# The sign of a double joined to its exponent: an integer and / or on VectorE in place of ScalarE's sign and a bf16 product

## The chip, the cores and the metric

The kernel runs on one core of a Trainium2 chip. The core has five engines that run side by side: TensorE (PE, matmuls, with its weight loads shown as PEld), VectorE (DVE), ScalarE (ACT), GpSimd (POOL) and SyncE (SP, which here issues the DMA transfers). The metric is device time in microseconds (us) of one launch, as the median of several runs. The profile of one further launch shows where that time goes.

## The reference

A recurrent attention over 768 steps feeds a gated feed-forward network. The matrices of the network are drawn as float64, so each of their numbers reaches the chip as 8 bytes.

```python
for t in range(S):                                   # B, H, S, D = 4, 8, 768, 40
    y[:, :, t] = np.einsum('bhd,bhde->bhe', rt, state)
    Sa = np.einsum('bhde,bhe->bhd', state, at)
    state_decay = state * wt[:, :, None, :] - np.einsum('bhd,bhe->bhde', Sa, bt)
    state = state_decay + np.einsum('bhd,bhe->bhde', vt, kt)
...
a = x @ w1                                           # x: 3072 x 320, w1, w2: 320 x 1024
b = x @ w2
h = a * b @ w3                                       # w3: 1024 x 1024
return (h @ w_out).astype(np.float32)                # w_out: 1024 x 320
```

## The kernel before

**Stages.** The sequence is cut into 12 chunks of 64 steps. Of each chunk the kernel makes: scaled inputs (`scale`: L438, L443, L459, L463, L467, L455), the products among its steps (`causal`: L492 on PE, `JP` and `lh` copies on ACT), the inverse of a triangular matrix on VectorE (`solve`: it begins with the transpose L524 and goes through some 50 products and sums, L550 and L554, to the transposes L599 and L602), the join of its halves (`join`: L625 and L632 on PE), then for four groups the recurrence itself (`rec`: L719, L726, L735, L748 on PE, L740, L772, L792 on VectorE), and at the end the network on the chunk's 256 tokens (`mlp`: `xs` is split into two parts by L827 and L830, L844 is x times w1 and w2, L858 the product of the two, L861 and L205 its two parts `gl` and `gh`, L870 the product with the last matrix).

**The weights' conversion.** Before the first `mlp` can start, the float64 weights have to become float32 on the chip. `convert` does this for a piece of 128 x 512 numbers; there are 31 pieces. A piece is loaded as 64-bit integers into `raw` (L317). L320 shifts the sign and exponent's 16 bits right by 4 and keeps 11 of them in `e`; L324 on ACT turns these into the bits of a bf16 power of two, still in `e`; L327 on ACT takes the sign of the 16-bit integer into `sg` (bf16); L330 and L334 on VectorE build the mantissa in `mf` (float32) from the two 32-bit halves; L338 multiplies sign and power (both bf16) into `sg`; L341 multiplies `mf` by it. What comes out is copied (`split`: ACT L205 and VectorE L383, L395 make the two parts of w1 and w2 in `W`), or feeds `product`, which multiplies w3 and w_out on PE once (L405, eight times 8 products) and splits the result into `W3h` and `W3l` (L205 and L410). The last pieces of `W` release the marker `W12`, which the first `xs` and L844 wait for.

**What sets the order.** Every engine works off one fixed list. `Order.place` makes these lists before the launch: it goes through all operations with a cost and a due time each, gives each to its engine at the earliest free time, picks by due time among those that can start, and gives out buffers (`SLOTS`) in the same pass. Operations with `two=True` are kept from running on VectorE and POOL at the same time in that plan. Strings in `ON` say for each piece whether L338 (`cb`, 26 d and 5 p) and L341 (`cv`, 9 d and 22 p) go to VectorE (d) or POOL (p). A changed cost or dependency in `convert` therefore changes the order of everything near it.

Of the kernel before, what the change touches and what calls it, by code (L numbers as in the profile page):

```python
# [8 lines left out]
F32 = mybir.dt.float32  # L9
F32R = mybir.dt.float32r  # L10
BF16 = mybir.dt.bfloat16
U16, I16 = mybir.dt.uint16, mybir.dt.int16
I32, U32, I64 = mybir.dt.int32, mybir.dt.uint32, mybir.dt.int64
AF = mybir.ActivationFunctionType
ALU = mybir.AluOpType
# [14 lines left out]
CW = 512  # L30
LAT = dict(pe=0.33, act=0.09, dve=0.09, pool=0.1, sp=2.4, nil=0.0)
SLOTS = dict(rc=2, fm=8, al=4, lh=6, gi=2, gt=1, ab=1, TDX=1, rv=3, xu=3, bk=3, hs=2, st=2, y=1, xr=1, JP=2, TT=2, bank=6,
             raw=4, e=3, sg=3, mf=4, w3f=3, xs=1, gh=1, gl=1, ga=2, o=2)


ENGINES = tuple(getattr(mybir.EngineType, n) for n in ("PE", "Activation", "DVE", "Pool", "SP"))
# [2 lines left out]
         ga=6.52, ml=90.63, kp=1.61, mt=25.46, mg=10.0)  # L39

ON = dict(cv="ppdpppdppppdddppppdpppppdddpppp", ws="d", lh="pppppppppppp", xs="dppppppppppp", gl="ppppppppppdd",
          cb="dddddddddddddddddddpdpddddddppp")
# [15 lines left out]
class Order:  # L58
# [11 lines left out]
    def slot(self, pool):  # L70
        return Slot(self, pool)

    def op(self, eng, cost, due, fn, r=(), w=(), two=False, kind=None, hold=(), dma=0.0):
        if self.direct:
            fn()
            return
        n, deps = len(self.ops), set()
        for k in r:
            deps.add(self.written.get(k))
            self.read.setdefault(k, []).append(n)  # L80
        for k in w:
# [112 lines left out]
def attention_moe(ctx: ExitStack, tc: tile.TileContext, fmx, fma, rv, vt, sq, svr, w12, w12c, w3t, wo, out):  # L194
    nc = tc.nc
    pe, act, dve, pool = nc.tensor, nc.scalar, nc.vector, nc.gpsimd
# [15 lines left out]
    for q in range(2):  # L212
        r = slice(64 * q, 64 * q + 64)
# [55 lines left out]

    cv, pp = ExitStack(), ExitStack()  # L270
    cvp = cv.enter_context(tc.tile_pool(name="cv", bufs=1, side="right"))
    for name, n, dt in (("raw", CW, I64), ("e", CW, U16), ("sg", CW, BF16), ("mf", CW, F32)):
        tiles[name] = [cvp.tile([128, n], dt, name=f"{name}{i}") for i in range(SLOTS[name])]
    ppp = pp.enter_context(tc.tile_pool(name="pp", bufs=1))
    wof = ppp.tile([128, NJ, DM], F32, name="wof")
# [16 lines left out]
    op, slot = order.op, order.slot  # L292
# [16 lines left out]
    def convert(src, dst, due, w=()):  # L309

        n = src.shape[1]
        raw, e, sg, mf = slot("raw"), slot("e"), slot("sg"), slot("mf")
        k = count[0]
        count[0] += 1

        def f1():
            sp.dma_start(out=raw.t[:, 0:n], in_=src)  # L317

        def f2():
            dve.tensor_scalar(out=e.t[:, 0:n], in0=raw.t.bitcast(U16)[:, 3:4 * n:4], scalar1=4, scalar2=0x7FF,  # L320
                              op0=ALU.logical_shift_right, op1=ALU.bitwise_and)

        def f3():
            act.activation(e.t[:, 0:n], e.t[:, 0:n], AF.Relu, scale=128.0, bias=ebias)  # L324

        def f4():
            act.activation(sg.t[:, 0:n], raw.t.bitcast(I16)[:, 3:4 * n:4], AF.Sign)  # L327

        def f5():
            dve.tensor_scalar(out=mf.t.bitcast(I32)[:, 0:n], in0=raw.t.bitcast(I32)[:, 1:2 * n:2], scalar1=0xFFFFF,  # L330
                              scalar2=0x100000, op0=ALU.bitwise_and, op1=ALU.bitwise_or)

        def f6():
            dve.scalar_tensor_tensor(out=mf.t[:, 0:n], in0=raw.t.bitcast(U32)[:, 0:2 * n:2], scalar=2.0 ** -32,  # L334
                                     in1=mf.t.bitcast(I32)[:, 0:n], op0=ALU.mult, op1=ALU.add)

        def f7(x):
            x.tensor_tensor(out=sg.t[:, 0:n], in0=sg.t[:, 0:n], in1=e.t[:, 0:n].bitcast(BF16), op=ALU.mult)  # L338

        def f8(e):  # L340
            e.tensor_tensor(out=mf.t[:, 0:n] if dst is None else dst(), in0=mf.t[:, 0:n], in1=sg.t[:, 0:n], op=ALU.mult)  # L341

        op("sp", 0.4, due - 8, f1, w=[raw], dma=2.0)
        op("dve", 0.42, due, f2, r=[raw], w=[e], two=True)
        op("act", 0.73, due, f3, w=[e])
        op("act", 0.67, due, f4, r=[raw], w=[sg])
        op("dve", 0.38, due, f5, r=[raw], w=[mf], two=True)
        op("dve", 0.62, due, f6, r=[raw], w=[mf], two=True)
        both(ON["cb"][k], 1.2, 0.38, due, f7, r=[e], w=[sg])
        both(ON["cv"][k], 1.25, 0.62, due, f8, r=[sg, "conv"], w=[mf] if dst is None else [mf, *w])  # L350
        return mf

    def weights():

        due, step = P["w0"], P["ws"]
        for k in range(3):
            if k == 1:
                for f in range(NJ * DM // CW):
                    cs = slice(CW * f, CW * f + CW)
                    convert(wo[:, cs], lambda cs=cs: wof.rearrange("p j n -> p (j n)")[:, cs], due, w=["wof"])  # L360
                    due += step
                for ib in range(NJ):
                    w3f = slot("w3f")
                    for f in range(1024 // CW):
                        cs = slice(CW * f, CW * f + CW)
                        convert(w3t[ib, :, cs], lambda w3f=w3f, cs=cs: w3f.t[:, cs], due, w=[(w3f, f)])
                        due += step
                    product(ib, w3f, due)
                op("nil", 0.0, due, second, w=["reg2"])
            for f in range(2048 // CW if k < 2 else DFF // CW):  # L370
                cs = slice(CW * f, CW * f + CW)
                due = split(k, f, cs, due)
                due += step
        op("nil", 0.0, due, third, r=[("W", k, f) for k in range(3) for f in range(4)], w=["W12", "conv"])

    def split(k, f, cs, due):

        over = ["conv"] if k == 0 else ["conv", "reg2"]
        if k < 2:
            mf = convert(w12[k * 128:k * 128 + 128, cs], None, due)  # L380

            def f2(e):
                e.tensor_tensor(out=WT[2 + k][:, cs], in0=mf.t, in1=WT[k][:, cs], op=ALU.subtract)  # L383

            op("act", 0.65, due, lambda: copy(WT[k][:, cs], mf.t), r=[mf, *over], w=[("W", k, f)])
            both(ON["ws"], 1.35, 0.62, due, f2, r=[mf, *over], w=[("W", k, f)])
            return due
        mf = convert(w12c[:, cs], None, due)
        for h in range(2):
            q, dst = slice(64 * h, 64 * h + 64), slice(DFF * h + CW * f, DFF * h + CW * f + CW)  # L390
            key = ("W", 2, 2 * h + f)
            for o in range(h + 1):
                op("act", 0.65, due, lambda q=q, dst=dst, o=o: copy(WT[4][64 * o:64 * o + 64, dst], mf.t[q]),
                   r=[mf, *over], w=[key])
            both(ON["ws"], 1.35, 0.62, due, lambda e, q=q, dst=dst: e.tensor_tensor(  # L395
                out=WT[4][64:128, dst], in0=mf.t[q], in1=WT[4][q, dst], op=ALU.subtract), r=[mf, *over], w=[key])
        return due
# [557 lines left out]
    for i in list(nc.cur_bb.bb.instructions)[begun:]:  # L955
        if i.engine in ENGINES:
            if i.engine in behind:
# [10 lines left out]
                      op1=ALU.is_equal)  # L968
# [78 lines left out]
```

## Time and profile before

| | |
|---|---|
| median of 3 runs | 756.51 us (756.47 to 760.34) |
| the profiled execution | 756.74 us, of which the span from first to last instruction 755.0 us |
| PE busy | 608.8 us (81%) |
| VectorE busy | 579.6 us (77%) |
| ACT busy | 480.3 us (64%) |
| POOL busy | 290.7 us (39%) |

The span is what the engines' rows cover; the 1.7 us beyond it lie around it. In the prediction's rows, a group of instructions reads: line, engine, operation, names written and read, shapes, how many, then busy time in us, the mean duration of one in ns, and the idle time before them with what ended it. A row of the timeline begins with its start in us and its duration in us; an instruction's successor on the same engine can start before that duration is over, so the step from start to start is what a row costs its engine.

### The profile page before, as it was taken

What the parts mean: (1) busy time and instruction counts of PE and PEld (TensorE: products, weight loads), DVE (VectorE), ACT (ScalarE), POOL (GpSimd) and SP (SyncE); (2) the same over time, 40 slices, a digit from 0 to 9 for tenths busy, and PEclk for the clock granted to TensorE, in tenths of its full rate; (3) what the DMA queues carried; (4) which work ended last, traced back from release to release, by engine and by line L of the source; (5) the groups of instructions that cost most, each with busy time, mean ns of one, the idle gap of its engine ahead of it and who ended that gap; (6) DMA issues with size and microseconds to landing.
All of it is one profiled execution on the core that took longest, in us unless ns stands there. A gap on an engine that the chain in (4) does not pass through costs nothing.

```text
span 755.0 us, 23802 instructions
## 1 busy us (share of the span) xinstructions
PE 608.8 (81%) x9458; PEld 525.1 (70%) x9458; DVE 579.6 (77%) x1317; ACT 480.3 (64%) x1309; POOL 290.7 (39%) x374
## 2 busy tenths in 40 slices
PE   1312199658689899898898998998989989999996
PEld 1211176336579788797787887977878779788996
DVE  6969999899885895985968959859589498693421
ACT  3744466458857668768676687686767776836431
POOL 3155414534443363443533634435426244321000
PEclk9999999877779999999999999999999999999999
DMA  7833264134220312313113233142232231211010
GB/s 181 223 90 96 81 184 143 44 123 135 62 51 15 97 51 70 88 44 98 50 51 96 50 74 83 46 97 53 54 89 57 63 80 46 55 28 44 8 35 20
DMA packets 67554, 57.63 MB, mean 76 GB/s; under 512 B 31600, under 2 KB 58480, under 8 KB 67440
## 3 DMA queue, kind: packets, MB, share of 16 engines
q1 hardware_dynamic: 67440, 56.08, 27.9%
q8 instruction: 76, 1.25, 0.7%
q14 instruction: 38, 0.31, 0.1%
HBM read 47.40 MB, written 3.93 MB: 68 GB/s over the span
## 4 chain that ended last, share of the span: by engine, by line
DVE 31%; PE 21%; ACT 18%; issue 6%; SPq 3%; DMA 1%; POOL 0%; DVEq 0%; ACTq 0%; POOLq 0%
PE bank L844 8%; DVE tmp L550 6%; ACT JP L205 5%; ACT TT L205 4%; DVE xu L740 3%; PE bank L870 3%; PE bank L748 3%; SPq L802 3%; PE bank L492 2%; DVE ab L524 2%; DVE DG L554 2%; ACT xu L205 2%; DVE fm L443 2%; DVE ga L858 2%; DVE Tp L554 2%
## 5 line engine op out<-in xcount | busy, mean ns | idle before, releaser
L844 PE MATMUL bank<-xs,W 128*128 128x256 f32 x1536 | 205.5, 288 | 2.3 <-issue 1.7
L844 PEld LDWEIGHTS bank<-xs,W 128*128 128x128 f32 x1536 | 188.4, 190 | 10.3 <-issue 3.7
L740 DVE TENSOR_TENSOR xu<-bank,mask_h 64x208 f32<-64x208 f32 x192 | 71.2, 371 | 57.7 <-PE bank L735 54.5
L467 POOL TENSOR_TENSOR fm<-fm,gi 104x512 f32<-104x512 f32 x44 | 62.7, 1425 | 117.0 <-DVE gi L463 91.2
L205 ACT ACTIVATE xu<-bank 64x128 f32<-64x128 f32 (+2 forms) x368 | 90.7, 297 | 19.0 <-PE bank L669 9.2
L205 ACT ACTIVATE JP<-bank 32x256 f32<-32x256 f32 (+1 forms) x216 | 75.7, 350 | 38.2 <-PE bank L492 34.8
L510 POOL TENSOR_SCALAR_AFFINE_SELECT lh<-lh 64x256 f32<-64x256 f32 x96 | 39.9, 415 | 129.6 <-ACT lh L205 125.8
L455 POOL TENSOR_TENSOR lh<-al,fm 104x512 f32<-104x512 f32 x48 | 59.5, 1245 | 43.5 <-PE bank L726 32.5
L748 PE MATMUL bank<-xu,bk 128*40 128x104 f32 (+1 forms) x768 | 49.6, 262 | 24.2 <-DVE xu L740 24.2
L726 PE MATMUL bank<-xu,lh 104*64 104x104 f32 (+2 forms) x768 | 53.2, 272 | 17.4 <-ACT xu L205 9.1
L861 POOL TENSOR_TENSOR gl<-ga,gh 128x512 fp32r<-128x512 f32 x40 | 51.5, 1286 | 32.8 <-ACT gh L205 32.8
L679 POOL TENSOR_SCALAR_AFFINE_SELECT xu<-xu 64x256 f32<-64x256 f32 x96 | 41.2, 429 | 57.7 <-ACT xu L205 49.6
L870 PE MATMUL bank<-W3h,gh 128*128 128x320 f32 x192 | 63.2, 329 | 0.0
L748 PEld LDWEIGHTS bank<-xu,bk 128*40 128x40 f32 (+1 forms) x768 | 37.4, 118 | 34.0 <-DVE xu L740 29.0
L726 PEld LDWEIGHTS bank<-xu,lh 128*64 128x64 f32 (+2 forms) x768 | 41.4, 145 | 27.9 <-ACT xu L205 16.5
L870 PE MATMUL bank<-W3l,gh 128*128 128x320 f32 x192 | 59.3, 309 | 0.0
L870 PE MATMUL bank<-W3h,gl 128*128 128x320 f32 x192 | 59.1, 308 | 0.0
L205 ACT ACTIVATE gh<-ga 128x512 fp32r<-128x512 f32 x48 | 30.1, 628 | 38.1 <-DVE ga L858 37.8
L447 ACT ACTIVATE gi<-fm 104x256 f32<-104x256 f32 x48 | 20.0, 416 | 53.7 <-DVE fm L443 51.2
L694 PE MATMUL bank<-ident,fm 104*128 104x104 f32 x192 | 28.8, 277 | 29.9 <-DMA al<-in_fma_dram 11.6
L405 PE MATMUL bank<-wof,w3f 128*128 128x320 f32 x128 | 44.2, 497 | 6.4 <-POOL w3f L341 6.2
L492 PE MATMUL bank<-lh,fm 40*64 40x64 f32 x1536 | 38.8, 238 | 12.8 <-POOL fm L467 8.3
(102 smaller groups left out, 1297.5 us busy)
## 6 DMA issues: line engine op xcount, KB each, us to landing
fm<-in_fmx_dram SPq DMA_DIRECT2D x48, 313.6 KB
raw<-in_w3t_dram SPq DMA_DIRECT2D x16, 512.0 KB
rv<-in_rv_dram SPq DMA_DIRECT2D x96, 80.0 KB
raw<-in_w_dram SPq DMA_DIRECT2D x8, 512.0 KB
al<-in_fma_dram SPq DMA_DIRECT2D x96, 40.0 KB
xu<-in_vt_dram SPq DMA_DIRECT2D x96, 40.0 KB
out_dram<-o SPq DMA_DIRECT2D x48, 80.0 KB
xr<-y SPq DMA_DIRECT2D x72, 40.0 KB
```

The lines of the kernel that those rows point to most:

```text
L205: act.activation(out_, in_, AF.Copy, scale=scale)
L405: pe.matmul(out=pt.t[:, 0:DM], lhsT=w[:, j], rhs=wof[:, j], start=(j == 0), stop=(j == NJ - 1))
L455: e.tensor_tensor(out=lh.t[0:104], in0=al.t.unsqueeze(1).to_broadcast(full), in1=gam(c, g)[:, :, 0:C].unsqueeze(1).to_broadcast(full), op= ...
L467: e.tensor_tensor(out=X, in0=X, in1=gi.t.unsqueeze(2).to_broadcast([104, NP, 2, C]), op=ALU.mult)
L492: pe.matmul(out=bank(ab)[64 * x:64 * x + 64, p], lhsT=X[r, p, x], rhs=lh.t[r, ab, p], start=True, stop=True)
L550: dve.tensor_tensor(out=scratch(*shape), in0=x().to_broadcast([128, *shape]), in1=y().to_broadcast([128, *shape]), op=ALU.mult)
L726: pe.matmul(out=view(hp)[64 * ab:64 * ab + 64, p], lhsT=lh.t[k, ab, p], rhs=xu.t[k, ab, p], start=True, stop=True)
L740: dve.tensor_tensor(out=xu.t[64 * ab:64 * ab + 64, ab, k:NP:2], in0=qs[ab].t[r, 256:256 + 2 * N].rearrange("p (n t) -> p n t", n=2), in1=m ...
L748: pe.matmul(out=q(r, p), lhsT=bk.t[:, p, r], rhs=xu.t[:, ab, p], start=(c == 0), stop=True, skip_group_check=True)
L844: pe.matmul(out=pt.t[:, TOK * x:TOK * x + TOK], lhsT=WT[k][:, cs], rhs=xs.t[:, z], start=(n == 0), stop=(n == 7))
L861: both(ON["gl"][c % NCH], 1.35, 0.62, t + 1, lambda e, a=a, j=j: e.tensor_tensor(out=gl.t[:, j:j + 2], in0=a.t, in1=gh.t[:, j:j + 2], op=A ...
L870: pe.matmul(out=pt.t[:, 0:DM], lhsT=l.t[:, j, ts], rhs=W3[r][:, j], start=(j == 0 and n == 0), stop=(j == NJ - 1 and n == 2))
```

## The change

`convert` keeps L320 (shift and mask) and L324 (the bf16 power of two). ACT's L327 and the tile `sg` go. In place of L338 there is one `scalar_tensor_tensor` on VectorE (L336 of the changed kernel) that takes the top 16 bits of each number from `raw`, ands them with 0x8000 and ors them into `e`. The final product (L340 of the changed kernel) reads `e` as bf16 instead of `sg`. All 31 of the new instructions are on VectorE; `cb` is no longer read. `e` has four buffers in place of three, and each is held until the final product. Line numbers of the changed kernel are smaller from here on: L330 has become L327, L334 L331, L341 L340, and after `convert` each is smaller by 1.

```diff
-             raw=4, e=3, sg=3, mf=4, w3f=3, xs=1, gh=1, gl=1, ga=2, o=2)
+             raw=4, e=4, mf=4, w3f=3, xs=1, gh=1, gl=1, ga=2, o=2)
...
-        def f4():
-            act.activation(sg.t[:, 0:n], raw.t.bitcast(I16)[:, 3:4 * n:4], AF.Sign)
...
-        def f7(x):
-            x.tensor_tensor(out=sg.t[:, 0:n], in0=sg.t[:, 0:n], in1=e.t[:, 0:n].bitcast(BF16), op=ALU.mult)
-
-        def f8(e):
-            e.tensor_tensor(out=mf.t[:, 0:n] if dst is None else dst(), in0=mf.t[:, 0:n], in1=sg.t[:, 0:n], op=ALU.mult)
+        def f7():
+
+            dve.scalar_tensor_tensor(out=e.t[:, 0:n], in0=raw.t.bitcast(U16)[:, 3:4 * n:4], scalar=0x8000,
+                                     in1=e.t[:, 0:n], op0=ALU.bitwise_and, op1=ALU.bitwise_or)
+
+        def f8(x):
+            x.tensor_tensor(out=mf.t[:, 0:n] if dst is None else dst(), in0=mf.t[:, 0:n],
+                            in1=e.t[:, 0:n].bitcast(BF16), op=ALU.mult)
...
-        op("act", 0.67, due, f4, r=[raw], w=[sg])
...
-        both(ON["cb"][k], 1.2, 0.38, due, f7, r=[e], w=[sg])
-        both(ON["cv"][k], 1.25, 0.62, due, f8, r=[sg, "conv"], w=[mf] if dst is None else [mf, *w])
+        op("dve", 0.62, due, f7, r=[raw], w=[e], two=True)
+        both(ON["cv"][k], 1.25, 0.62, due, f8, r=[e, "conv"], w=[mf] if dst is None else [mf, *w])
```

The lists of all engines change up to the third chunk's network. Three places show how.

VectorE's list early in the conversion (names are tiles with buffer numbers), before:

```order
L467 TENSOR_TENSOR fm_99<-fm_99,gi_115 104x512
L338 TENSOR_TENSOR sg_168<-sg_168,e_165 128x512
L320 TENSOR_SCALAR e_166<-raw_162 128x512
L330 TENSOR_SCALAR mf_172<-raw_162 128x512
L334 SCALAR_TENSOR_TENSOR mf_172<-raw_162,mf_172 128x512
L338 TENSOR_TENSOR sg_169<-sg_169,e_166 128x512
```

and the same place now:

```order
L466 TENSOR_TENSOR fm_99<-fm_99,gi_115 104x512
L336 SCALAR_TENSOR_TENSOR e_165<-raw_161,e_165 128x512
L320 TENSOR_SCALAR e_166<-raw_162 128x512
L327 TENSOR_SCALAR mf_170<-raw_162 128x512
L331 SCALAR_TENSOR_TENSOR mf_170<-raw_162,mf_170 128x512
L442 SCALAR_TENSOR_TENSOR fm_100<-fm_100,first 104x260
L336 SCALAR_TENSOR_TENSOR e_166<-raw_162,e_166 128x512
```

L336 stands where L338 stood, with `raw` as an input more, and a scan of the next group (L442) has moved between the two.

VectorE's list where the weights are done and the first `xs` is made (row 376 of it before), before:

```order
L772 TENSOR_TENSOR st_130<-bank_154,fm_103 104x80
L395 TENSOR_TENSOR W_4_1599<-mf_173,W_4_1599 64x512 x2
L459 TENSOR_TENSOR gt_116<-fm_100,gi_114 104x256
L463 SCALAR_TENSOR_TENSOR gi_114<-gt_116,gi_114 104x256
L443 SCALAR_TENSOR_TENSOR fm_101<-fm_101,first 104x260
L830 TENSOR_TENSOR xs_1852<-xr_132,xs_1852 128x768
L792 TENSOR_TENSOR y_131<-bank_156,fm_103 104x2x64
L792 TENSOR_TENSOR y_131<-bank_154,fm_103 104x2x64
```

and now (row 388):

```order
L771 TENSOR_TENSOR st_130<-bank_157,fm_103 104x80
L791 TENSOR_TENSOR y_131<-bank_156,fm_103 104x2x64
L791 TENSOR_TENSOR y_131<-bank_157,fm_103 104x2x64
L549 TENSOR_TENSOR tmp<-ab,DG 128x256
L394 TENSOR_TENSOR W_4_1512<-mf_171,W_4_1512 64x512 x2
L458 TENSOR_TENSOR gt_116<-fm_101,gi_115 104x256
L462 SCALAR_TENSOR_TENSOR gi_115<-gt_116,gi_115 104x256
L442 SCALAR_TENSOR_TENSOR fm_102<-fm_102,first 104x260
L829 TENSOR_TENSOR xs_1852<-xr_132,xs_1852 128x768
```

Counted over the whole list ahead of the first `xs`, seven instructions that stood behind it stand ahead of it now: one each of L443, L459, L463, L550 and L554 (256 elements) and two L792; all else is the same but for `convert`'s own. On PE, sixteen L492 rows have moved ahead of the first L844 in the same way.

PE's list at the join of the chunk whose recurrence follows the second `mlp`, before:

```order
L870 MATMUL bank_156<-W3h,gl_1851 128x320
L632 MATMUL bank_155<-TDX_117,JP_134 32x32 x32
L870 MATMUL bank_156<-W3h,gh_1850 128x320
L870 MATMUL bank_156<-W3l,gh_1850 128x320
L870 MATMUL bank_156<-W3h,gl_1851 128x320
L870 MATMUL bank_156<-W3h,gh_1850 128x320
L870 MATMUL bank_156<-W3l,gh_1850 128x320
L870 MATMUL bank_156<-W3h,gl_1851 128x320
L719 MATMUL bank_153<-rv_118,SB 64x104
```

and now:

```order
L869 MATMUL bank_156<-W3h,gh_1850 128x320
L869 MATMUL bank_156<-W3l,gh_1850 128x320
L869 MATMUL bank_156<-W3h,gl_1851 128x320
L631 MATMUL bank_155<-TDX_117,JP_134 32x32 x32
L718 MATMUL bank_152<-rv_118,SB 64x104
```

The six products between the join's second half and the recurrence's first step have moved ahead. From that L719 on, the kinds and sizes of instructions on PE stand in the same order in both kernels to the end (4623 matmuls of 6164); so they do on VectorE (807 of 1309), ACT and POOL from near the same point, and every list has the same instructions ahead of it but for `convert`'s.

More of the change, by code (lines that the diff above doesn't have):

```diff
@@ L271, in attention_moe @@
     cvp = cv.enter_context(tc.tile_pool(name="cv", bufs=1, side="right"))
-    for name, n, dt in (("raw", CW, I64), ("e", CW, U16), ("sg", CW, BF16), ("mf", CW, F32)):
+    for name, n, dt in (("raw", CW, I64), ("e", CW, U16), ("mf", CW, F32)):
         tiles[name] = [cvp.tile([128, n], dt, name=f"{name}{i}") for i in range(SLOTS[name])]
@@ L311, in convert @@
         n = src.shape[1]
-        raw, e, sg, mf = slot("raw"), slot("e"), slot("sg"), slot("mf")
+        raw, e, mf = slot("raw"), slot("e"), slot("mf")
         k = count[0]
```

## The prediction

> **What bounds the kernel.** I read the page's forty slices of the span first (18.9 us each, busy share in tenths):
>
> ```profile
> DVE  6969999899885895985968959859589498693421
> ```
>
> VectorE is near full in the first eleven, to about 210 us, but for the start and a stretch around 45 us, and has pauses after that. I then asked for the busy time of each engine in the stretches that the order of the work suggests: up to the first L844, from there to the point where both kernels' lists agree, and the rest.
>
> ```profile
> core 0: us, PE busy (x) PEld busy (x) DVE busy (x) ACT busy (x) POOL busy (x), PEclk, DMA share, GB/s
> 14.00:212.00 198.00, 106.29 (x1461) 78.79 (x1460) 178.56 (x367) 119.33 (x299) 80.08 (x91) 0.90 0.41 119
> 212.00:292.00 80.00, 75.14 (x1167) 68.08 (x1171) 61.86 (x133) 54.40 (x147) 36.54 (x43) 0.96 0.21 54
> 292.00:755.00 463.00, 425.54 (x6834) 376.91 (x6826) 329.12 (x794) 302.95 (x857) 168.40 (x217) 1.00 0.24 59
> ```
>
> Up to 212 us VectorE is busy 178.6 of 198 us (90%), while ACT has 40% and POOL 60% to spare. Then PE takes over (94%, then 92%). VectorE's timeline shows the handover, from the last `W` part (L395) over `xs` (L830) into the next chunk's solve,
>
> ```profile
> 209.68 1.41 DVE L395 TENSOR_TENSOR W<-mf,W 64x512 fp32r<-64x512 f32 x2
> 211.11 0.43 DVE L459 TENSOR_TENSOR gt<-fm,gi 104x256 f32<-104x256 f32 x1
> 211.57 0.42 DVE L463 SCALAR_TENSOR_TENSOR gi<-gt,gi 104x256 f32<-104x256 f32 x1
> 211.92 0.69 DVE L443 TENSOR_TENSOR_SCAN fm<-fm,first 104x260 f32<-104x260 f32 x1
> 212.53 0.93 DVE L830 TENSOR_TENSOR xs<-xr,xs 128x768 fp32r<-128x768 f32 x1
> 213.38 0.48 DVE L792 TENSOR_TENSOR y<-bank,fm 104x128 f32<-104x128 f32 x2
> 213.77 0.42 DVE L554 TENSOR_REDUCE ab<-tmp 128x32 f32<-128x256 f32 x1
> 214.22 0.42 DVE L550 TENSOR_TENSOR tmp<-ab,DG 128x256 f32<-128x256 f32 x1
> 214.68 0.42 DVE L554 TENSOR_REDUCE Tp<-tmp 128x32 f32<-128x256 f32 x1
> ```
>
> and PE's, whose L844 `xs` releases:
>
> ```profile
> 213.51 3.57 PE L844 MATMUL bank<-xs,W 128*128 128x256 f32 x15 [0.57 <-DVE xs L830]
> ```
>
> The conversion lies wholly ahead of this point. Behind the join at 292 us the two kernels' lists agree on the compute engines, so the 463 us from there should stay what they are, and the forecast is by how much that point moves.
>
> **The change part by part.** The costs are read as steps from start to start of undisturbed rows in one stretch:
>
> ```profile
> 25.01 0.42 DVE L338 TENSOR_TENSOR sg<-sg,e 128x512 bf16<-128x512 bf16 x1
> 25.35 0.42 DVE L320 TENSOR_SCALAR e<-raw 128x512 uint16<-128x512 uint16 x1
> 25.68 0.42 DVE L330 TENSOR_SCALAR mf<-raw 128x512 int32<-128x512 int32 x1
> 26.14 0.69 DVE L334 SCALAR_TENSOR_TENSOR mf<-raw,mf 128x512 f32<-128x512 uint32 x1
> 26.75 0.42 DVE L338 TENSOR_TENSOR sg<-sg,e 128x512 bf16<-128x512 bf16 x1
> ```
>
> and the groups of the stretch from 14 to 212 us:
>
> ```profile
> L334 DVE SCALAR_TENSOR_TENSOR mf<-raw,mf 128x512 f32<-128x512 uint32 x31 | 29.7, 959 | 0.9
> L330 DVE TENSOR_SCALAR mf<-raw 128x512 int32<-128x512 int32 x31 | 18.7, 603 | 0.0
> L320 DVE TENSOR_SCALAR e<-raw 128x512 uint16<-128x512 uint16 x31 | 17.0, 552 | 2.1 <-DMA raw<-in_wo_dram 1.1 <-DMA raw<-in_w_dram 1.0
> L338 DVE TENSOR_TENSOR sg<-sg,e 128x512 bf16<-128x512 bf16 x26 | 11.9, 458 | 3.8 <-ACT e L324 2.4 <-ACT sg L327 1.4
> ...
> L327 ACT ACTIVATE sg<-raw 128x512 bf16<-128x512 int16 x31 | 20.2, 661 | 5.0 <-DVE w3f L341 1.6 <-DMA raw<-in_w_dram 1.4 <-POOL mf L341 1.2
> ```
>
> *The old product on VectorE becomes the and / or.* L338 costs 25.35 - 25.01 = 0.34 us. The new instruction is of L334's operation, with 512 elements from two tensors in SBUF, but 16-bit; no row shows that form. Bounds: 0.34 (L338, also two 16-bit tensors of 512) and 0.61 (L334, 26.75 - 26.14). I take 0.61, since L334 is the same operation. 26 x (0.61 - 0.34) = +7.0 us; the lower end is 0. [...]
>
> *The five products that POOL made come to VectorE:* 5 x 0.61 = +3.1 us (1.7 at the lower bound).
>
> *POOL loses them.* A POOL product can hold VectorE up:
>
> ```profile
> 129.38 1.15 POOL L338 TENSOR_TENSOR sg<-sg,e 128x512 bf16<-128x512 bf16 x1 [4.71 <-DVE mf L334]
> 129.43 1.39 DVE L459 TENSOR_TENSOR gt<-fm,gi 104x256 f32<-104x256 f32 x1
> ...
> 147.08 2.75 DVE L334 SCALAR_TENSOR_TENSOR mf<-raw,mf 128x512 f32<-128x512 uint32 x1
> 148.13 1.15 POOL L338 TENSOR_TENSOR sg<-sg,e 128x512 bf16<-128x512 bf16 x1
> ```
>
> L459 takes 0.43 us at 211.11, so 1.0 us was lost beside the first product; L334 lost 2.75 - 0.69 = 2.06 us, and I give half of that to the second, which covers the row's later part. The other three stand beside VectorE rows of their usual length. So -2.0 us. New collisions of L336 itself bound this from above: the stretch's L334 rows lose (0.959 - 0.69) x 31 = 8.3 us, and if L336 lost as much, the term would be +6.3. [...]
>
> *ACT loses 31 signs, 20.2 us.* ACT is no limit here, so this pays only where VectorE waited for ACT:
>
> ```profile
> DVE ab L524 <- ACT JP L205: 4.0, 1, 4.0
> DVE sg L338 <- ACT e L324: 2.4, 2, 1.4
> DVE sg L338 <- ACT sg L327: 1.4, 2, 1.0
> ...
> DVE W3l L410 <- ACT W3h L205: 1.1, 1, 1.1
> ```
>
> (us in total, times, longest). The 1.4 us for `sg` go. The waits for `e`, `JP` and `W3h` hang on ACT's queue only in part: `e` comes from L320 through L324 as before, and the JP copies wait for PE. I take half of `e`'s: in all -2.6; bounds 0, if other waits take their place, and -8.9, all four rows.
>
> *Seven rows moved ahead of `xs`* (L459, L463, L443, twice L792, L550, L554). From start to start in the handover's rows above, they cost 0.46 + 0.35 + 0.61 + 0.39 + 0.46 + 0.45 = 2.7 us, by which `xs` and L844 come later. It isn't lost work: VectorE has it behind itself afterwards, and PE's sixteen L492 rows too.
>
> ```profile
> 224.09 0.69 PE L492 MATMUL bank<-lh,fm 40*64 40x64 f32 x32
> ```
>
> (one such group, 32 passes). If PE sets the time from 212 to 292 us, 2.7 - 0.7 = 2.0 stay; if VectorE's solve of the next chunk does, none. PE's join has also lost products that filled its pauses:
>
> ```profile
> 291.29 0.31 PE L870 MATMUL bank<-W3l,gh 128*128 128x320 f32 x1
> 291.44 0.30 PE L870 MATMUL bank<-W3h,gl 128*128 128x320 f32 x1
> ```
>
> Six at 0.15 us from start to start make up to 0.9 us of pause. Between 0 and 2.9 I take +1.0.
>
> *`e` held longer* costs nothing while it has a fourth buffer; what would be queued behind a missing one is L320 and with it ACT's L324. The loads of `raw` keep their four buffers, whose last reader is now L336 instead of L327 or L334; the idle before L320 in the groups above, 2.1 us for two loads, is what loads cost now, and I leave it.
>
> **Sum:** 7.0 + 3.1 - 2.0 - 2.6 + 1.0 = +6.5 us on the profiled execution's 756.74 us, that is 763.2; the median of the runs is 0.2 below that execution, so 763.0.
>
> **The rivals.** *Within half a per cent (753 to 760).* If the 16-bit and / or runs at L338's 0.34, the first term is 0 and the second 1.7, and the sum 1.7 - 2.0 - 2.6 + 1.0 = -1.9, so 754.6; with 0.61 but all of ACT's 8.9 us recovered it is 763.0 - 6.3 = 756.7. Against the first stands L334, against the second that only the 1.4 us name the sign.
>
> *Faster: the new lists avoid POOL's collisions.* The place is `convert`'s three kinds of rows. Above 0.69 (L334) and 0.42 us (L330, L320) each, they lose 8.3 + 31 x (0.603 - 0.42) = 5.7 and 31 x (0.552 - 0.42) = 4.1, in all 18.1 us. The plan keeps `two` operations apart and was made anew. If three quarters (13.6) vanish, the time is 763.0 - 13.6 = 749.4; it is under 752.7 from 10.3 us on. For it speaks that POOL has five instructions less; against it that 22 L341 and all of L455 and L467 stay on POOL.
>
> [...]
>
> *The change doesn't do what it says:* if the conversion were hidden, nothing would move. VectorE's 90% up to 212 us and L844's wait for `xs` speak against it.
>
> **How the numbers follow.** About 0.5% (3.8 us) is what a measurement of this kernel can tell from no change. Forecast 0.60, with 760.3 to 771 as its own range: the upper end is what comes out with POOL's term at +4 instead of -2.0 and most of ACT's -2.6 gone. Within half a per cent 0.24, far slower 0.03, faster 0.10; nothing moves 0.03. Slower than +0.5% are 0.60 and 0.03, so 0.63; same 0.27; faster 0.10. The range leaves out the far slower rival and most of the faster one: 754 to 771.
>
> **What would show it.** Right: L844 first at about 221 us instead of 212, the stretch from the join to the end still 463 us, L336 at 0.61 to 0.69 us, VectorE at 90% or more up to `xs`. Wrong: L336 at 0.42 us; idle before L524 or L336 much smaller or larger than 4.0 and 3.8 us; L334, L330 and L320 with means nearer to 0.69 and 0.42 us; or a join that waits long after `xs` has come.

## The result and the profile after

The changed kernel takes 765.6 us (median of 4 runs, 765.0 to 766.2) against 756.8 us before. The measured ratio is 1.0107, with a 95% interval of 1.008 to 1.0134; by it the change costs 8.1 us, while the two medians lie 8.9 us apart. The forecast was 763.0 us. Every run below was timed beside runs of the kernel before on its own chip. The kernel before had medians of 757.0 to 757.5 us there, so ratios are what is compared.

The profiled execution of the changed kernel took 764.99 us, 763.3 of it in the span. First its forty slices (18.9 us before, 19.1 us now):

```profile
DVE  7999899999994695894986958959679589593431
PEclk9999999767569999999999999999999999999999
```

VectorE is full for one slice longer, and the stretch of low shares around 45 us is gone. Next the same three stretches as before. The first ends where the first `xs` releases PE and the second at the join:

```profile
14.00:219.10 205.10, 108.52 (x1497) 80.61 (x1497) 192.99 (x384) 104.10 (x277) 82.51 (x90) 0.86 0.40 117
219.10:297.30 78.20, 73.31 (x1120) 66.95 (x1119) 57.76 (x125) 50.97 (x137) 32.74 (x39) 0.97 0.19 50
297.30:763.30 466.00, 427.17 (x6844) 378.62 (x6838) 329.30 (x794) 303.30 (x857) 167.89 (x216) 0.99 0.23 59
```

VectorE is busy 193.0 of 205.1 us (94%, was 90%). The last stretch is 466 us long, where 463 stood before. PE's timeline has the two points between them (L843 is the old L844, L718 the old L719):

```profile
220.24 2.07 PE L843 MATMUL bank<-xs,W 128*128 128x256 f32 x8 [1.03 <-DVE xs L829]
297.34 0.94 PE L718 MATMUL bank<-rv,SB 40*64 40x104 f32 x32
```

L843 behind the wait for `xs` comes 6.7 us later than before (220.24 against 213.51; one L843 ahead of that wait 6.2 us, 218.63 against 212.39), L718 5.7 us (297.34 against 291.67), and the end of the span 8.3 us (763.3 against 755.0). VectorE's groups from 14 to 222 us:

```profile
L331 DVE SCALAR_TENSOR_TENSOR mf<-raw,mf 128x512 f32<-128x512 uint32 x31 | 28.0, 905 | 1.0
L336 DVE SCALAR_TENSOR_TENSOR e<-raw,e 128x512 uint16<-128x512 uint16 x31 | 24.5, 795 | 1.4 <-ACT e L324 1.3
L327 DVE TENSOR_SCALAR mf<-raw 128x512 int32<-128x512 int32 x31 | 15.0, 483 | 0.0
L320 DVE TENSOR_SCALAR e<-raw 128x512 uint16<-128x512 uint16 x31 | 14.1, 459 | 0.0
L442 DVE TENSOR_TENSOR_SCAN fm<-fm,first 104x260 f32<-104x260 f32 x13 | 13.8, 1074 | 0.0
```

L336 takes 24.5 us, where the old product's 26 took 11.9 on VectorE: 12.6 more. The means of L331, L327 and L320 are smaller than before (905, 483 and 459 ns against 959, 603 and 552), but that of the scan L442 is larger (1074 against 920 ns). VectorE's longest waits in the same stretch:

```profile
DVE xu L739 <- PE bank L734: 3.4, 2, 2.0
DVE e L336 <- ACT e L324: 1.3, 1, 1.3
DVE fm L437 <- DMA fm<-in_fmx_dram: 0.7, 1, 0.7
```

The 4.0 us ahead of L524 (now L523), the waits for the sign and those for `raw` are gone. From its first instruction to the first `xs`, and counting pauses of 0.15 us or more, VectorE idled 9.0 us, against 16.7 before.

### The profile page after: what moved, and what is told of

Its sections match the earlier page's. It is cut to its first block, busy times and chain, and to the rows that moved or that the text cites. A ratio compares the mean times of both kernels' runs of the same rounds, so it can differ in the third digit from the quotient of the medians.

```text
span 763.3 us, 23753 instructions
## 1 busy us (share of the span) xinstructions
PE 610.0 (80%) x9458; PEld 526.8 (69%) x9458; DVE 590.1 (77%) x1322; ACT 462.0 (61%) x1278; POOL 290.1 (38%) x369
## 4 chain that ended last, share of the span: by engine, by line
DVE 43%; PE 29%; ACT 16%; issue 6%; DMA 3%; SPq 2%; POOL 0%; DVEq 0%; ACTq 0%; POOLq 0%
PE bank L843 9%; DVE tmp L549 7%; ACT JP L205 4%; PE bank L869 4%; ACT TT L205 3%; DVE fm L442 3%; DVE xu L739 3%; PE bank L747 3%; DVE ab L523 3%; PE bank L404 3%; PE bank L491 3%; DVE DG L553 3%; PE bank L725 2%; DVE mf L331 2%; DVE e L336 2%
## 5 line engine op out<-in xcount | busy, mean ns | idle before, releaser
L843 PE MATMUL bank<-xs,W 128*128 128x256 f32 x1536 | 205.8, 288 | 2.9 <-ACT xs L826 1.7
L843 PEld LDWEIGHTS bank<-xs,W 128*128 128x128 f32 x1536 | 188.7, 190 | 11.0 <-ACT xs L826 2.1
L739 DVE TENSOR_TENSOR xu<-bank,mask_h 64x208 f32<-64x208 f32 x192 | 71.3, 371 | 65.8 <-PE bank L734 62.6
L509 POOL TENSOR_SCALAR_AFFINE_SELECT lh<-lh 64x256 f32<-64x256 f32 x96 | 43.3, 451 | 116.2 <-ACT lh L205 111.8
L725 PE MATMUL bank<-xu,lh 128*64 128x104 f32 (+2 forms) x768 | 55.5, 280 | 19.2 <-POOL xu L678 9.3
L725 PEld LDWEIGHTS bank<-xu,lh 128*64 128x64 f32 (+2 forms) x768 | 43.6, 150 | 30.1 <-ACT xu L205 16.1
L869 PE MATMUL bank<-W3h,gh 128*128 128x320 f32 x192 | 62.9, 327 | 0.0
L869 PE MATMUL bank<-W3h,gl 128*128 128x320 f32 x192 | 59.3, 309 | 0.2 <-POOL gl L860 0.2
L869 PE MATMUL bank<-W3l,gh 128*128 128x320 f32 x192 | 59.2, 308 | 0.0
L857 DVE TENSOR_TENSOR ga<-bank,ga 128x512 f32<-128x512 f32 x48 | 32.9, 684 | 22.2 <-PE bank L843 19.5
L404 PE MATMUL bank<-wof,w3f 128*128 128x320 f32 x128 | 42.1, 479 | 7.2 <-POOL w3f L340 7.2
L624 PE MATMUL bank<-TDX,JP 32*32 32x32 f32 x768 | 15.8, 199 | 40.1 <-DVE TDX L601 40.1
```

The lines of the kernel that those rows point to most:

```text
L404: pe.matmul(out=pt.t[:, 0:DM], lhsT=w[:, j], rhs=wof[:, j], start=(j == 0), stop=(j == NJ - 1))
L509: pool.affine_select(out=lh.t[q, ab], in_=lh.t[q, ab], pattern=[[0, NP], [1, C]], compare_op=ALU.is_gt, fill=0.0, base=0, channel_multipli ...
L725: pe.matmul(out=view(hp)[64 * ab:64 * ab + 64, p], lhsT=lh.t[k, ab, p], rhs=xu.t[k, ab, p], start=True, stop=True)
L739: dve.tensor_tensor(out=xu.t[64 * ab:64 * ab + 64, ab, k:NP:2], in0=qs[ab].t[r, 256:256 + 2 * N].rearrange("p (n t) -> p n t", n=2), in1=m ...
L843: pe.matmul(out=pt.t[:, TOK * x:TOK * x + TOK], lhsT=WT[k][:, cs], rhs=xs.t[:, z], start=(n == 0), stop=(n == 7))
L869: pe.matmul(out=pt.t[:, 0:DM], lhsT=l.t[:, j, ts], rhs=W3[r][:, j], start=(j == 0 and n == 0), stop=(j == NJ - 1 and n == 2))
```

## The experiments

"Its own order" means that every engine's list is that of the kernel named, row for row but for the edit.

**e1: the longer instruction in the old order.** The kernel before:

```diff
+            if x is dve:
+                dve.scalar_tensor_tensor(out=sg.t[:, 0:n], in0=sg.t[:, 0:n], scalar=1.0, in1=e.t[:, 0:n].bitcast(BF16),
+                                         op0=ALU.mult, op1=ALU.mult)
+                return
             x.tensor_tensor(out=sg.t[:, 0:n], in0=sg.t[:, 0:n], in1=e.t[:, 0:n].bitcast(BF16), op=ALU.mult)
```

> The kernel before with its own order on every engine; only the 26 products of sign and exponent on VectorE (L338) are issued as scalar_tensor_tensor (sign times 1.0 times exponent) instead of tensor_tensor. ScalarE's sign stays. Theory A (VectorE sets the time up to xs, so a longer instruction there carries one to one, whatever the order): if the form costs what the changed kernel's L336 costs (0.65 to 0.69 us against 0.34), the time rises by 26 x 0.31 to 0.35 = 8.1 to 9.1 us, to 764.8 to 765.9 against 756.7. Rival B (the 8.9 us of the change come from the new order that was planned around it, the seven rows ahead of xs and the join without its filler, and not from the instruction): within 2 us of 756.7. If the form runs at 0.34 us on bf16 operands, both expect no change, and the run only tells that the types and not the form cost the time.

Measured: 766.7 us, ratio 1.0129 (1.0105 to 1.0152); the profiled execution's span is 762.5 us, 7.5 more. VectorE's timeline:

```profile
26.32 0.68 DVE L339 SCALAR_TENSOR_TENSOR sg<-sg,e 128x512 bf16<-128x512 bf16 x1
26.93 0.42 DVE L320 TENSOR_SCALAR e<-raw 128x512 uint16<-128x512 uint16 x1
```

and the group of all 26:

```profile
L339 DVE SCALAR_TENSOR_TENSOR sg<-sg,e 128x512 bf16<-128x512 bf16 x26 | 19.1, 734 | 3.2 <-ACT e L324 2.2 <-ACT sg L327 1.0
```

The step is 26.93 - 26.32 = 0.61 us, where it was 0.34. Summed from start to start over the 26, waits left out, VectorE spends 17.6 us on it instead of 10.5, so 7.1 more. The first `xs` starts 6.9 us later (219.47 against 212.53) and the span ends 7.5 us later. Theory A holds: with no sign moved, nothing taken from POOL and the old order kept, the longer form alone costs as much as the whole change. The types of the and / or are not needed for it, since these operands are bf16.

**e2: the short instruction in the new order.** The changed kernel:

```diff
-            dve.scalar_tensor_tensor(out=e.t[:, 0:n], in0=raw.t.bitcast(U16)[:, 3:4 * n:4], scalar=0x8000,
-                                     in1=e.t[:, 0:n], op0=ALU.bitwise_and, op1=ALU.bitwise_or)
+            eb = e.t[:, 0:n].bitcast(BF16)
+            dve.tensor_tensor(out=eb, in0=eb, in1=eb, op=ALU.max)
```

> The changed kernel with its own order on every engine; only L336, all 31 of them, is replaced by a tensor_tensor maximum of the exponent with itself on bf16 operands (0.34 us in the kernel before). It leaves out the sign of the weights. Theory A (the duration of the step carries one to one): 765.6 less 31 x 0.34 to 0.40 (the step's mean in the changed kernel is 0.738) = 10.5 to 12.4, so 753.2 to 755.1, below the kernel before by the relief on ScalarE and POOL. Rival B (the new order costs the time): 762 or more, since the order is untouched. The stretch from the first rows behind the third xs to the end was 470.5 us in the changed kernel and 468.9 before: A expects it to stay at 470 or so here, because the join is still without its filler.

Measured: 761.0 us, ratio 1.0047 (1.0031 to 1.0063). That is neither theory's number. The group of VectorE from 14 to 222 us:

```profile
L337 DVE TENSOR_TENSOR e<-e 128x512 bf16<-128x512 bf16 x31 | 16.3, 529 | 1.9 <-ACT e L324 1.8
```

and its longest wait there:

```profile
DVE xu L739 <- PE bank L734: 6.5, 4, 3.4
```

The rows got shorter by 24.5 - 16.3 = 8.2 us, but L739 now waits 6.5 us for PE instead of 3.4, and VectorE's idle time up to `xs` grew from 9.0 to 13.1 us. So in the new order the longer form costs 0.0107 - 0.0047 = 0.6% or 4.5 us (the two profiled executions lie 5.9 us apart). Something in that order holds the other 0.47% (3.6 us), though neither the longer form nor the sign on ScalarE is there any more. From the third `xs` to the end this execution takes 469.8 us, about the 470 that theory A expected.

**e3: no sign on ScalarE, old order.** The kernel before, with L327 not issued and a constant tile of ones, which POOL fills once (those lines are not shown), in its place:

```diff
-            act.activation(sg.t[:, 0:n], raw.t.bitcast(I16)[:, 3:4 * n:4], AF.Sign)
+            pass
...
-            x.tensor_tensor(out=sg.t[:, 0:n], in0=sg.t[:, 0:n], in1=e.t[:, 0:n].bitcast(BF16), op=ALU.mult)
+            x.tensor_tensor(out=sg.t[:, 0:n], in0=plus[:, 0:n], in1=e.t[:, 0:n].bitcast(BF16), op=ALU.mult)
```

> The kernel before with its own order; ScalarE's sign (L327, 31 of them) is not issued, and L338 multiplies a constant tile of ones by the exponent in its place, with the form and duration of before. It leaves out the sign of the weights. This is the relief on ScalarE alone. The prediction took 2.6 us for it (all of L338's waits on the sign, 1.4, and half of the e waits, 1.2): 754.1. Theory A (as the changed kernel's idle times of VectorE suggest, 16.7 us before against 9.0 after up to xs): up to 7.7 us, so 749 to 752. Rival B (ScalarE's queue is no limit, the waits move to something else): 756 to 757.

Measured: 759.0 us, ratio 1.0026 (1.0015 to 1.0037): 2.0 us slower, where every expectation had no change or a gain. VectorE's waits from 14 to 222 us:

```profile
DVE ab L526 <- ACT JP L205: 4.5, 2, 4.0
DVE sg L340 <- ACT e L326: 3.6, 2, 2.6
DVE xu L742 <- PE bank L737: 3.1, 1, 3.1
DVE e L322 <- DMA raw<-in_wo_dram: 2.0, 1, 2.0
```

The 1.4 us for the sign are gone, and the waits for `e` (2.4 before), for PE at L742 (1.0) and for `raw` grew by more. The 4.0 us ahead of the transpose stay, so in the old order they do not hang on the sign. VectorE's idle time up to `xs` is 21.2 us instead of 16.7.

**e4: both edits of e1 and e3, old order.**

```diff
-            act.activation(sg.t[:, 0:n], raw.t.bitcast(I16)[:, 3:4 * n:4], AF.Sign)
+            pass
...
+            if x is dve:
+                dve.scalar_tensor_tensor(out=sg.t[:, 0:n], in0=plus[:, 0:n], scalar=1.0, in1=e.t[:, 0:n].bitcast(BF16),
+                                         op0=ALU.mult, op1=ALU.mult)
+                return
...
```

> The kernel before with its own order on every engine; ScalarE's sign is not issued, and the 26 products on VectorE are scalar_tensor_tensor (ones times 1.0 times exponent), as the two edits of the runs beside it together; POOL keeps its five. It leaves out the sign of the weights. Theory A (durations add): the sum of the two edits run alone, 757 + 8.6 - 2.6 to 7.7, so 758 to 763. What the changed kernel's 765.6 has over this is then the new order, the other buffers and the five instructions that moved from POOL to VectorE (5 x 0.68 = 3.4 by their duration). Rival B (relief on ScalarE is worth nothing once VectorE is later): the same as the first run.

Measured: 764.3 us, ratio 1.0103 (1.0079 to 1.0127), which lies between theory A's 763 and e1's 766.7 and decides for neither. The first wait in VectorE's list is still

```profile
DVE ab L530 <- ACT JP L205: 4.2, 2, 4.0
```

and its idle time up to `xs` is 16.8 us, as before the change. With the short form the sign's removal cost 0.26%; with the long form it read 1.0103 against 1.0129, and those two intervals overlap. So in the old order no gain from it shows. The 7.7 us by which the changed kernel idles less therefore do not come from ScalarE's relief alone. They come with its new order and the fourth buffer of `e`, which no run takes apart, and no run puts the sign back into that order.

**e5: the and / or twice.** The changed kernel, with L336 issued a second time:

```diff
             dve.scalar_tensor_tensor(out=e.t[:, 0:n], in0=raw.t.bitcast(U16)[:, 3:4 * n:4], scalar=0x8000,
                                      in1=e.t[:, 0:n], op0=ALU.bitwise_and, op1=ALU.bitwise_or)
+            dve.scalar_tensor_tensor(out=e.t[:, 0:n], in0=raw.t.bitcast(U16)[:, 3:4 * n:4], scalar=0x8000,
+                                     in1=e.t[:, 0:n], op0=ALU.bitwise_and, op1=ALU.bitwise_or)
```

> The changed kernel with its own order; L336 is issued twice in a row for each of the 31 pieces (the second and/or with the same bits changes nothing in the result). Theory A (VectorE's durations carry one to one up to xs): 31 x 0.684 = 21.2 us more, so about 786.8; less by what idle time of VectorE (9.0 us up to xs) takes up, at the least 777.8. Rival B (the step is partly hidden in this order): the run with the short step moved VectorE's sum by 8.2 us but xs by 5.6, a share of 0.68; by that 14.4 us more, about 780.

Measured: 789.6 us, ratio 1.0429 (1.0411 to 1.0446), 24 us above the changed kernel. The second issue (L338) in the groups up to 246 us:

```profile
L338 DVE SCALAR_TENSOR_TENSOR e<-raw,e 128x512 uint16<-128x512 uint16 x31 | 27.3, 881 | 1.1
```

Of its 27.3 us of busy time, 24 reach the end. That is theory A, somewhat above its 786.8, with a mean of 881 ns instead of 684. That the difference comes from meeting POOL's work is argued from the rows above and not shown by this run.

**e8: no product on VectorE.** The kernel before in its own order:

```diff
+            if x is dve:
+                return
             x.tensor_tensor(out=sg.t[:, 0:n], in0=sg.t[:, 0:n], in1=e.t[:, 0:n].bitcast(BF16), op=ALU.mult)
```

> The kernel before with its own order; the 26 products of sign and exponent on VectorE (L338) are not issued at all, ScalarE's sign is. It leaves out the exponent of the weights in those pieces. This is what joining the sign for nothing would bring. Theory A (one to one): 26 x 0.403 = 10.5 us less, 746.7. Rival B (below the time of before another engine or a transfer sets the stretch up to xs, since a kernel with the sign off ScalarE gained nothing): a gain under 4 us, 753 or more.

Measured: 747.9 us, ratio 0.9879 (0.9862 to 0.9896), 9.2 us less. The 26 steps had 10.5 us. PE's products with `xs` behind the wait for it:

```profile
204.82 1.44 PE L846 MATMUL bank<-xs,W 128*128 128x256 f32 x5 [1.13 <-DVE xs L832]
```

They come 8.7 us earlier than at 213.51, the `xs` on VectorE itself 9.5 us earlier (203.07 against 212.53). So in the old order VectorE's steps ahead of `xs` count almost one to one in both directions, and these 9.2 us are what joining the sign at no cost on those 26 pieces would bring.

**e7: the five products of POOL on VectorE.** The kernel before, with the order planned anew:

```diff
-          cb="dddddddddddddddddddpdpddddddppp")
+          cb="ddddddddddddddddddddddddddddddd")
```

> The kernel before with the five products of sign and exponent that POOL had given to VectorE by the table of numbers; sign, form and types stay, but the order is planned anew with it. The prediction took 5 x 0.34 = 1.7 for the five and -2.0 for POOL's lock, so -0.3: 756.9. Theory A (the runs so far: VectorE's durations carry, the lock only changes place): +1.7 or a little more by collisions, 758.9 to 760. Rival B (POOL's relief counts in full): down to 749.

Measured: 760.3 us, ratio 1.0043 (1.0027 to 1.0059), 3.3 us slower. VectorE's group from 14 to 222 us:

```profile
L338 DVE TENSOR_TENSOR sg<-sg,e 128x512 bf16<-128x512 bf16 x31 | 16.0, 516 | 7.5 <-ACT sg L327 7.5
```

and its longest wait from 14 to 240 us:

```profile
DVE sg L338 <- ACT sg L327: 7.5, 4, 4.4
```

The rows grew from 11.9 to 16.0 us, more than the 1.7 us that five at 0.34 make, and in this plan L338 waits 7.5 us for ScalarE's sign. That wait belongs to this plan and not to the changed kernel. The plan has also put thirteen other VectorE rows behind the first `xs`, which so comes 1.1 us earlier than before (211.45 against 212.53), while the way from there to the third `xs` takes 77.4 us instead of 73.5. So the run does not price the five. It shows no gain such as rival B's.

**The join.** What was left to explain was e2's 3.6 us. In the changed kernel PE's timeline at the join reads:

```profile
295.60 0.24 PE L631 MATMUL bank<-TDX,JP 32*32 32x32 f32 x2 [0.78 <-ACT JP L205]
296.21 1.19 PE L631 MATMUL bank<-TDX,JP 32*32 32x32 f32 x62 [0.37 <-ACT JP L205]
...
299.04 3.61 PE L725 MATMUL bank<-xu,lh 128*64 128x104 f32 x32 [0.76 <-ACT xu L205]
```

and the busy time of the engines by 2 us (after the stretch and its length: PE, PEld, DVE, ACT and POOL, then granted clock, DMA share, GB/s):

```profile
298.00:300.00 2.00, 1.10 (x19) 0.65 (x12) 0.00 (x0) 1.93 (x7) 0.00 (x0) 0.81 0.27 63
300.00:302.00 2.00, 2.00 (x28) 2.00 (x25) 0.00 (x0) 1.48 (x5) 0.65 (x1) 0.50 0.35 85
```

PE in the kernel before, at the same place in its work (L726 is now L725; the 16 products between the two rows are left out):

```profile
292.81 0.39 PE L726 MATMUL bank<-xu,lh 128*64 128x104 f32 x2 [0.19 <-ACT xu L205]
...
294.56 0.93 PE L726 MATMUL bank<-xu,lh 104*64 104x104 f32 x14 [0.18 <-ACT xu L205]
```

and its busy times:

```profile
288.00:292.00 4.00, 4.00 (x96) 3.58 (x98) 0.86 (x3) 3.89 (x9) 0.73 (x1) 1.00 0.01 4
292.00:296.00 4.00, 3.43 (x78) 2.66 (x70) 0.00 (x0) 3.66 (x12) 2.15 (x3) 1.00 0.35 90
```

and of e2, whose join begins at 288 us:

```profile
292.00:296.00 4.00, 3.96 (x78) 3.29 (x76) 0.00 (x0) 2.93 (x9) 0.09 (x1) 0.50 0.35 86
```

Before, the products leave no pause at the join above 0.19 us, and the clock stays at 1.00. Now PE pauses for 0.78, 0.37 and 0.76 us, the clock falls to 0.50, and L725 lasts 3.6 us, where the same matmuls ran from 292.81 to about 295.5. Other kernels with one of these two orders agree in this: with the old order (e1, e8) the clock stays at 1.00 at this join, with the new one (e2) it falls to 0.50. Four runs go after this.

**e6: the filler put back.** The changed kernel, with eighteen L869 moved behind L624 and L631 on PE's list (the text below is put ahead of the loop that issues the list):

```diff
...
+    for o, behind in ((pq[i - 1], pq[i]), (pq[i - 2], pq[i]), (pq[i + 1], pq[i + 2])):
+        placed.remove(o)
+        placed.insert(placed.index(behind) + 1, o)
```

> The changed kernel; on PE alone eighteen products of the mlp (L869) are issued later: twelve from ahead of the first block of the join (L624) to behind it, and the six between L624 and L631 to between L631 and L718, so that 12 and 6 fill the pauses as they did before the change. Nothing else moves. Theory A (the missing filler lets PE pause at the join, and the stretch from the first rows behind the third xs to the end is longer by the 1.5 to 2.6 us that it is longer than before): 1.5 to 2.6 us less, 763.0 to 764.1. Rival B (PE waits there for ScalarE's copies in any case, the products only move): 765.6, within 0.5. Rival C (L624 and with it the chain of the join starts later, or the products now delay L718): up to 1.8 us more.

Measured: 768.0 us, ratio 1.0132 (1.0108 to 1.0156): no gain, but a loss at about the upper end of rival C. PE's timeline:

```profile
293.44 1.85 PE L624 MATMUL bank<-TDX,JP 32*32 32x32 f32 x64 [1.93 <-DVE TDX L601]
...
304.49 3.61 PE L725 MATMUL bank<-xu,lh 128*64 128x104 f32 x32 [0.36 <-ACT xu L205]
```

and the clock:

```profile
292.00:294.00 2.00, 0.56 (x25) 0.59 (x27) 2.00 (x6) 1.55 (x3) 0.80 (x1) 0.89 0.00 0
294.00:296.00 2.00, 2.00 (x52) 1.94 (x47) 0.73 (x2) 1.91 (x6) 0.00 (x0) 0.50 0.03 8
...
308.00:310.00 2.00, 2.00 (x61) 1.97 (x64) 0.85 (x3) 0.61 (x2) 1.18 (x1) 0.50 0.31 94
```

The twelve had been covering a wait that I had overlooked, L624's for VectorE's `TDX`. Without them PE stands still for 1.93 us, and the clock is at 0.50 for the next 17 us, through the very filler that was put back. The pause was moved, not filled.

**e9 to e11: more filler, and none.** e9 is the changed kernel once more. e10 is the changed kernel with two times five extra products into an idle PSUM tile (`pq` is PE's list, `i` the place of this join's L624 in it):

```diff
...
+    def fill():
+        for _ in range(5):
+            pe.matmul(out=tiles["ab"][0][:, 0:DM], lhsT=W3[0][:, 0, 0:128], rhs=W3[0][:, 0], start=True, stop=True)
+
+    for o in (pq[i + 1], pq[i + 4]):
+        placed.insert(placed.index(o) + 1, dict(fn=fill))
```

e11 is the kernel before without the filler (`thin` is set while this join's filler is issued):

```diff
...
                     for n, (l, r) in enumerate(((gh, 0), (gh, 1), (gl, 0))):
+                        if thin and (j, n) != (NJ - 1, 2):
+                            continue
...
```

> The changed kernel itself, unaltered, beside the next two on the same chip, so that small differences at the join can be read against it. Both theories expect 765 to 766, and in its trace a pause of PE at the join of the chunk behind the second mlp (some 2 us in all between L624 and L725) with the granted clock at 0.5 some 4 us later.

> The changed kernel; on PE alone two times five products of the size of L869 (128x320) are added at that join, between L869 and L631 and between L718 and L725, into a PSUM tile that nobody reads then. They fill pauses of 0.78 and 0.37, and of 0.76 us with 0.15 us each, and the kernel's work is untouched. Theory A (PE's pauses there bring the granted clock down, and the low clock makes L725 and what follows longer): the clock stays 1.00 at the join, L725 takes about 2.6 us instead of 3.6, and the stretch from the first rows behind the third xs to the end falls from 470.5 to 468 or 469; the time is 1 to 2.5 us below the changed kernel's beside it. Rival B (the clock falls for another reason, such as the small 32x32 blocks): no change in the clock, and the time the same or up to 0.5 us longer.

> The kernel before with its own order; at the same join the eighteen products between L625, L632 and L719 are left out but for the one that closes the group, so that PE has the pauses that the changed kernel has there. It leaves out these products of one block of the last product of one chunk. Theory A (pauses bring the clock down): the granted clock falls to 0.5 within a few us of the join, where it was 1.00, and the stretch from the first rows behind the third xs to the end, 468.9 before, grows by 1 to 3 us although PE has 2.5 us less to do. Rival B (the pauses cost nothing by themselves): the clock stays 1.00 and the stretch stays or gets shorter, by at most 2.5 us.

Measured: e9 765.1 us, ratio 1.0112 (1.0092 to 1.0132); e10 762.5 us, 1.0072 (1.0056 to 1.0088); e11 758.0 us, 1.0017 (1.0003 to 1.0032). e9's clock at the join:

```profile
296.00:298.00 2.00, 1.64 (x61) 1.64 (x62) 0.07 (x1) 1.08 (x3) 1.27 (x1) 0.54 0.01 3
298.00:300.00 2.00, 1.96 (x43) 1.57 (x38) 0.00 (x0) 1.66 (x4) 0.00 (x0) 0.50 0.52 125
300.00:302.00 2.00, 2.00 (x20) 1.71 (x22) 0.00 (x0) 1.79 (x7) 0.00 (x0) 0.50 0.20 48
```

e10's PE:

```profile
295.71 0.89 PE L957 MATMUL ab<-W3h 128*128 128x320 f32 x5
...
300.19 1.48 PE L725 MATMUL bank<-xu,lh 128*64 128x104 f32 x18
301.86 0.93 PE L725 MATMUL bank<-xu,lh 104*64 104x104 f32 x14 [0.19 <-ACT xu L205]
```

and its clock:

```profile
298.00:300.00 2.00, 2.00 (x65) 1.83 (x59) 0.00 (x0) 1.47 (x5) 0.33 (x1) 1.00 0.35 86
300.00:302.00 2.00, 1.72 (x23) 1.13 (x24) 0.00 (x0) 1.95 (x8) 0.31 (x1) 1.00 0.36 86
```

Work that computes nothing made the kernel faster. The clock stays at 1.00, L725 ends 301.86 + 0.93 - 300.19 = 2.6 us after it starts, and the next solve's transpose begins 15.5 us after the third `xs` (309.36 and 293.82) instead of 17.0 in e9 (309.90 and 292.92). The time falls by 1.0112 - 1.0072 = 0.4%, 3.0 us; the two intervals do not meet. About half of that is seen in the rows at the join. These 3.0 us are not what the join had lost, though: the same distance from the third `xs` to the transpose is 16.0 to 16.1 us in the kernels with the old order (before, e1, e3, e4, e8) and 16.5 to 17.1 in those with the new one (the changed kernel, e2, e5, e9). So the loss at the join is 0.5 to 1.0 us in the rows, and e10 comes out below the old order too. e11 is the mirror, in PE's timeline:

```profile
288.62 0.24 PE L633 MATMUL bank<-TDX,JP 32*32 32x32 f32 x2 [1.02 <-ACT JP L205]
```

and in the clock:

```profile
288.00:290.00 2.00, 1.01 (x36) 0.90 (x38) 0.03 (x1) 1.92 (x5) 0.00 (x0) 0.87 0.00 0
290.00:292.00 2.00, 2.00 (x49) 1.66 (x48) 0.85 (x2) 1.96 (x6) 0.72 (x1) 0.50 0.03 8
```

Seventeen products less, and the clock that was 1.00 falls to 0.50. The next transpose starts at 303.07 instead of 302.06, and the whole is 1.3 us slower although PE has 2.5 us less to do. In this one profiled execution, the fastest of its twelve, the stretch from the third `xs` to the end was 1.2 us shorter and not longer, against theory A; the later chunks gave that back, and I have no cause for it. So it is shown that without the filler the clock falls at this join; that this makes the whole kernel longer rests on the times of the runs alone.

## Why the prediction was right, and where its steps were not

The forecast of +6.5 us (763.0) met +8.1 us. Its range and its direction held, but several terms were wrong and made up for one another, so that the total came out this close is in part luck. Some of its own signs of being wrong came in: the idle time ahead of L524 went from 4.0 us to none, that ahead of the new step from 3.8 to 1.4, and L330's and L320's means moved towards 0.42 us.

*The price of the new instruction was right.* 26 x 0.27 = 7.0 us was forecast; e1's rows give 7.1 us, and carry to the end. L336 lasts 0.684 us in the median, close to L334's 0.693, and takes nearly twice the step of L338 (0.60 us from 21.68 to 22.28 against 0.34), which would have made the rival within half a per cent come true. Nothing far slower, which the prediction gave 0.03, shows in these rows: L336 is not above L334. The types make no difference that the traces show: with two bf16 sources the form takes 0.68 to 0.69 us a row in e1 (24 to 30 us), with two uint16 ones 0.684 us in the median in the changed kernel.

*That the conversion sets the time was right.* VectorE is at 94%, and e5 and e8 show the slope. The first L843 was called at about 221 instead of 212 us; like for like it came at 218.63 instead of 212.39, so 6.2 us later and not 9.

*ScalarE's relief, -2.6, was wrong.* e3 shows +2.0 us, e4 nothing that differs. The step that failed is the reading of a wait's end as its cause: what ended last was the sign, but with the sign gone the waits for `e`, PE's bank and the load came out longer by more than its 1.4 us (e3). The 4.0 us ahead of L524, which were in my bounds, stay without the sign in the old order (e3, e4) and are gone in the new one.

*The relief from POOL's five products, -2.0, does not show as a gain.* L331, L327 and L320 lost less than before by their means, but L336, whose mean lies 795 - 684 = 111 ns above its median (L338's lay 458 - 418 = 40 ns above), and the scans (1074 against 920 ns) lost more. e7 gave +3.3 us, not -0.3, though its new plan moved other rows as well. Such losses change place from run to run: in e5 the means of L331, L320 and the scans are 840, 575 and 800 ns instead of 905, 459 and 1074, in a list that is the same but for the second L336. No run prices the +3.1 for the five either.

*The join, +1.0 for the seven rows and the filler together, was too small, and it was put at the wrong end.* The seven rows stand ahead of L843 and can only be part of those 6 to 7 us. The filler's loss lies behind the join, where I said that 463 us would stay; there were 466, of which about 1 us is only that L718 now comes sooner behind the third `xs` (4.6 against 5.7 us). I had counted six products as moved. PE's timelines show eighteen: twelve ran between L625 and L632 and six behind, where now six run between L624 and L631 and none behind. And I had counted pauses of up to 0.9 us, but not a PE clock of 0.50 behind them (the changed kernel, e9, e11). e10's filler, with which the clock stays at 1.00, brings 3.0 us.

By the ratios, 4.5 of the 8.1 us in the new order are the longer form (e2). Of the other 3.6 us, 0.5 to 1.0 are seen in the rows at the join, and e11, which takes the filler out of the old order, costs 1.3 us. What is left, some 2 us or more, is all the rest together: the sign gone, the five products, the seven rows, and no run takes it apart. Each of these is a difference of two ratios and good to some 2 us. In the old order the longer form alone costs 7.5 (span) to 9.8 us (ratio), so the new order also hides some of it. Which of its moved rows does that is open; I did not move the seven rows back, since their consumers would have had to move as well.

## What to carry to other kernels

Merging two cheap operations into one is no gain when the merged form takes nearly twice the step of what it replaces on the engine that sets the time (0.60 against 0.34 us here), so compare steps on that engine first and count work saved on an engine with slack as nothing until a run shows otherwise (e3, with 31 signs less on ScalarE, was 2.0 us slower). Before counting a wait as recovered, look at what ends next behind it, and test it by taking the awaited work out and keeping the order. Filler on PE was worth more here than the pauses it fills (e10 gained 3.0 us, where the changed kernel's pauses at the join are 0.78, 0.37 and 0.76 us), so when a plan is made anew, compare what stands between the small products of its dependent chain.

## What was not expected of the hardware

PE's granted clock fell behind pauses far shorter than I would have guessed. In e9, 0.79 and 0.37 us without a matmul within 2 us are followed by 0.54 and 0.50 for some 7 us; e6's 1.93 us by 0.50 for 17 us. Added up from the granted clock of each 2 or 4 us, the low stretch at this join lasts 3.4 us in the changed kernel, 6.8 to 6.9 in e2, e9 and e11 and 17.1 in e6, which are about 1, 2 and 5 times 3.4 us. Pauses alone do not settle it, however, since in the kernel before

```profile
312.75 1.13 PE L748 MATMUL bank<-xu,bk 128*40 128x104 f32 x16 [1.51 <-DVE xu L740]
```

```profile
312.00:316.00 4.00, 2.71 (x28) 2.14 (x28) 3.82 (x13) 0.91 (x3) 1.51 (x1) 1.00 0.18 40
```

PE pauses for 1.51 us in one piece, is idle for 1.29 of these 4 us and keeps 1.00. From 225 us on and up to the last few us of the span, the kernel before shows no drop (1.00 from 225 to 752 us) and the changed kernel only the one beside the 32x32 blocks of this join, so the size of the products may count as well; that is a guess of mine. Nor is the clock low behind all such blocks and pauses. In the changed kernel's next join

```profile
347.28 0.24 PE L631 MATMUL bank<-TDX,JP 32*32 32x32 f32 x2 [0.66 <-ACT JP L205]
347.89 1.19 PE L631 MATMUL bank<-TDX,JP 32*32 32x32 f32 x62 [0.37 <-ACT JP L205]
```

the clock stays at 1.00 (346 to 354 us). What decides between the two joins, no run here takes apart.

The other surprise is that scalar_tensor_tensor on 512 elements took 0.684 us in the median for uint16 (L336), 0.68 to 0.69 a row for bf16 (e1) and 0.693 in the median for a uint32 with an int32 (L334), while tensor_tensor on bf16 took 0.418 (L338).
